# Ten of eighteen gather matrices made on ScalarE as reciprocal roots, and a first hop that adds both halves of a value while it scatters

## The chip, the cores and the metric

The kernel runs on one core of one Trainium2 chip. It is one launch on one core with these engines: TensorE (PE in the profile; PEld are its weight loads), VectorE (DVE), ScalarE (ACT), GpSimd (POOL) and SyncE (SP), which here mostly issues transfers. Each engine works through its own instructions in the order in which the program lists them. The metric is the time of the launch in device microseconds, as the median of several runs.

## The reference

The input is a graph with 10,000 nodes, 160,000 edges and 128 features per node, and seven propagations ("hops") followed by a small transformer block over the eight resulting tokens of each node:

```python
h = x
toks = [x]
for _ in range(7):
    msg = h[src] * deg_inv_sqrt[src, None] * deg_inv_sqrt[dst, None]
    h = _segment_sum(msg, dst, N)
    toks.append(h)
tok = jnp.stack(toks, axis=1)                      # (N, 8, D)
t = _layernorm(tok, axis=-1)
q, key, v = (jnp.einsum('nkd,de->nke', t, w) for w in (wq, wk, wv))
attn = _softmax(jnp.einsum('nkd,nld->nkl', q, key) * scale, axis=-1)
o = tok + jnp.einsum('nkd,de->nke', jnp.einsum('nkl,nld->nkd', attn, v), wo)
r = _layernorm(o, axis=-1)
alpha = _softmax(jnp.einsum('nkd,d->nk', r, w_r), axis=-1)
return jnp.einsum('nk,nkd->nd', alpha, o)
```

## The kernel before

**Representation.** The nodes form 79 blocks of 128. A hop is done by matrix products with zero-one matrices: for a block of destinations, TensorE first gathers the source rows of its edges and then scatters them, that is, adds them up by destination. The table of a hop (`tab`) holds each value as two f16 halves side by side, a leading part in columns 0 to 127 and the remainder in columns 128 to 255, so that a row has 256 columns. The edges of a block are sorted into cells of 32 places by the block of their source. Blocks 0 to 71 of the sources have a cell of their own each, four cells to a matrix, so there are `NG` = 18 gather matrices of 4 x 32 columns. One more scatter matrix (`NI` = 1) and an overflow matrix (`Sov`) take rows that are fetched from DRAM by index (`fetch`, lines 519 to 528).

**Stages.** (1) The first bucket pass (`pass_a`) counts and sorts the edges by destination block. (2) The second bucket pass takes the destination blocks in quads: `place` (lines 409 to 495) ranks the edges of four blocks into cells and writes their rows to DRAM (`srow`), and `matrices` (lines 497 to 516) makes the gather and scatter matrices of each block, stores them (`GSd`) for the later hops, and keeps them for the first hop, which runs in the same stage one quad later. (3) Hops two to seven read the stored matrices. (4) The attention follows.

**`matrices`.** For each block, SyncE reads the block's row of 2304 places to all 128 partitions (`rb`, one buffer, line 504). VectorE compares it with the partition number plus one (`pid1`), which gives the 18 gather matrices in one instruction of 2304 columns (line 511), and makes the 19 scatter matrices in another of 2432 columns (line 514). Then SyncE stores both (line 516). The transfer of the next row is issued after line 511.

**`block`.** A step gathers one or two matrices (line 580: four products of 32 columns of weights each, into a PSUM tile `p` of 128 x 512; there are three such tiles in the first hop), copies `p` to an f16 tile `e` on ScalarE (line 585) or VectorE (line 587, as a multiplication by a tile of ones), and two steps later scatters (line 556) with the scatter matrix as weights and `e` as the moving operand, into the accumulator `acc`. Nearly all copies of the first hop are ScalarE's; in later hops five of nine are. In the first hop `e` has a 257th column of ones, which counts the edges of each destination. When all 18 are added, the fetched rows follow (lines 542 to 569), VectorE adds the two halves of `acc` into `s` (line 571), and `fin` takes `s`. In the first hop `fin` is `fin1` (line 648): VectorE copies the count (line 649), ScalarE scales `s` for the next table (line 652) and for the token (line 623, into `r`, one buffer).

**Order.** The stage is written as three generators that are advanced in turn, 16 rounds to a quad (line 684 on): in each round a step of `place` of the next quad (in two rounds of three), a step of `matrices` (in one of four) and a step of the first hop of the quad before. The instructions get this order as their priority; a planner then fixes the order on each engine from its own estimates of times, moving forward what it takes to be ready. Transfers on SyncE's queue stand in order with their waits: the next row (line 504), the matrices (line 516), the token rows (line 627), the new table's rows (line 161).

Of the kernel before, what the change touches and what calls it, by code (L numbers as in the profile page):

```python
# [7 lines left out]
F32 = mybir.dt.float32  # L8
# [4 lines left out]
AF = mybir.ActivationFunctionType  # L13
ALU = mybir.AluOpType
# [5 lines left out]
NT = 79  # L20
NG = 18
NI = 1
CELL = 334
NK = 79
NR = 10240
# [14 lines left out]
class Hops:  # L40
    def __init__(self, ctx, dp, missing, tab, tc, x, src, dst, dis):
# [34 lines left out]
        self.one = cp.tile([128, 1], F32, name="one")  # L76
        V.memset(self.one, 1.0)
# [318 lines left out]
    def pb_open(self, c):  # L396
        tc, V = self.tc, self.nc.vector
        self.bwp = c.enter_context(tc.tile_pool(name="bw", bufs=2))
        self.bw1 = c.enter_context(tc.tile_pool(name="bw1", bufs=1))
        self.pU = c.enter_context(tc.tile_pool(name="pU", bufs=1, space=PSUM))  # L400
        self.psm = c.enter_context(tc.tile_pool(name="psm", bufs=1, space=PSUM))

        cp = self.bp
        es = cp.tile([NS, 4, NJ], I32, name="es")
        self.nc.gpsimd.iota(es, pattern=[[1, 4], [4, NJ]], base=0, channel_multiplier=-1)
        self.esel = cp.tile([NS, 4, NJ], F16, name="esel")
        V.tensor_scalar(self.esel, es, 0.0, None, op0=ALU.is_equal)

    def place(self, ts, got):

# [85 lines left out]

    def matrices(self, ts, dsl, W):

        nc, V = self.nc, self.nc.vector

        def row(t):
            rb = self.bw1.tile([128, 4 * NG * CAP], F16, name="rb")
            r1 = self.srow[t:t + 1, :]
            nc.sync.dma_start(rb, bass.AP(tensor=r1.tensor, offset=r1.offset, ap=[[0, 128], [1, 4 * NG * CAP]]))
            return rb

        rb = row(ts[0])
        yield
        for g, t in enumerate(ts):
            w = self.gsp.tile([128, (NJ + NG) * 128], F8, name="w")  # L510
            V.tensor_scalar(w[:, NJ * 128:], rb, self.pid1, None, op0=ALU.is_equal, saturate=False)  # L511
            if t != ts[-1]:
                rb = row(t + 1)
            V.tensor_tensor(w[:, :NJ * 128].rearrange("p (j d) -> p j d", d=128), dsl[:, g, :, None].to_broadcast([128, NJ, 128]),  # L514
                            self.iof1[:, None, :].to_broadcast([128, NJ, 128]), op=ALU.is_equal, saturate=False)
            nc.sync.dma_start(self.GSd[t], w)
            W.append(w)
            yield
# [11 lines left out]
    def block(self, t, w, tab, og, pend, lag, runs, first, evac, fin, lead=False, late=False, mid=None, ahead=None,  # L530
              after=None):

        nc, V, A, T, G = self.nc, self.nc.vector, self.nc.scalar, self.nc.tensor, self.nc.gpsimd
        m = 257 if first else 256
        acc = []


        def fetched(i, start=False, stop=False):  # L540
            W = w[:, (NG + i) * 128:(NG + i + 1) * 128] if i < NI else self.Sov[:, t, :]
            T.matmul(acc[0][:, :256], W, og[i], start=start, stop=stop)  # L542
            if first:
                T.matmul(acc[0][:, 256:257], W, self.ones16, start=False, stop=False)

        def begin():
            acc.append(self.pacc.tile([128, 512], F32, name="acc", tag="acc"))
            for i in range(NI if late else NI + 1):
                fetched(i, start=i == 0)

        def scat(e, jj):
            if not acc:
                acc.append(self.pacc.tile([128, 512], F32, name="acc", tag="acc"))
            for j in range(e.shape[1]):
                J = 2 * jj + j
                T.matmul(acc[0][:, :m], w[:, J * 128:(J + 1) * 128], e[:, j, :m], start=first and J == 0,  # L556
                         stop=J == NG - 1 and not (first or late))
                if first and J == 0 and not lead:
                    for i in range(NI):
                        fetched(i)  # L560

        def close():
            if first:
                if lead:
                    for i in range(NI):
                        fetched(i)
                T.matmul(acc[0][:, 256:257], self.Sov[:, t, :], self.ones16, start=False, stop=False)
            if first or late:
                T.matmul(acc[0][:, :256], self.Sov[:, t, :], og[NI], start=False, stop=True)  # L569
            s = self.fp.tile([128, 128], F32, name="s")  # L570
            V.tensor_reduce(s, acc[0][:, 0:256].rearrange("p (h d) -> p d h", h=2), axis=X, op=ALU.add)  # L571
            fin(t, s, acc[0])

        def gather(jj):
            n = min(2, NG - 2 * jj)
            p = self.pg.tile([128, 2, 2, 128], F32, name="p")
            for j in range(n):
                for q in range(4):
                    s = 4 * (2 * jj + j) + q
                    T.matmul(p[32 * q:32 * q + 32, j], w[:, NJ * 128 + s * CAP:NJ * 128 + (s + 1) * CAP], tab[:, s, :], start=True, stop=True)  # L580
            e = self.ebuf[self.eb_i % len(self.ebuf)]
            self.eb_i += 1
            pv = p[:, :n].rearrange("p j h d -> p j (h d)")
            if evac(jj):
                A.copy(e[:, :n, 0:256], pv)  # L585
            else:
                V.tensor_tensor(e[:, :n, 0:256], pv, self.one[:, :, None].to_broadcast([128, n, 256]), op=ALU.mult)  # L587
            pend.append(lambda: scat(e[:, :n], jj))

        jj = 0  # L590
        for i, n in enumerate(runs):
            for _ in range(n):
                gather(jj)
                if jj == 0 and not first and not mid:
                    ahead(self.ebuf[(self.eb_i - 1) % len(self.ebuf)][:, 0, 0:1])
                jj += 1
            if mid:
                mid(0)
            if not first:
                begin()  # L600
                if mid:
                    ahead()
            while len(pend) > lag:
                pend.pop(0)()
            if mid:
                mid(1)
            if after:
                after()
            if i == len(runs) - 1:
                pend.append(close)  # L610
            yield
# [17 lines left out]
    def run(self, ctx, att, nhop=K):  # L629
        tc, nc, V, A, T, G = self.tc, self.nc, self.nc.vector, self.nc.scalar, self.nc.tensor, self.nc.gpsimd  # L630
        with ExitStack() as c:
# [14 lines left out]


            def fin1(t, s, acc):
                V.tensor_copy(self.indeg[:, t:t + 1], acc[:, 256:257])  # L649
                if not done:  # L650
                    fin1.y = self.fp.tile([128, 2, 128], F32, name="y2")
                A.activation(fin1.y[:, len(done), :], s, AF.Copy, scale=self.dis2[:, t:t + 1])
# [25 lines left out]
            for q in range(nq + 1):  # L678
# [619 lines left out]
```

## Time and profile before

| | us |
|---|---|
| time, median of 3 runs (lowest, highest) | 3996.6 (3993.74, 4000.15) |
| the profiled execution, its own time | 3999.62 |
| its span, first to last instruction | 3997.8 |
| VectorE busy, second bucket pass, 600.30 to 1105.65 us | 492.02 of 505.35 |
| ScalarE busy, the same stretch | 316.19 |

In the rows of the profile an instruction is given by line, engine and operation, then output and input by the program's names with their shapes and types, then how often it occurs. "Mean ns" is the length of one, while busy time counts overlapping instructions once, so that a queue of instructions of one kind can stand closer than its mean. Idle time is the time of that engine just before the instruction, and the name behind the arrow is what ended it. The ends of matmuls are modelled, so a busy TensorE is not a TensorE at its peak.

### The profile page before, as it was taken

The page shows a single profiled execution, that of the slowest core. Times are in us where ns is not written, and L with a number is a line of the kernel's source. Part 1 is how long each engine was busy: PE and PEld are TensorE (multiplying, and loading weights), DVE is VectorE, ACT ScalarE, POOL GpSimd, SP SyncE. Part 2 cuts the span into 40 slices and gives each one's busy share as a digit, 9 for nine tenths or more (in the row PEclk, how much of TensorE's full clock was granted, in tenths as well). Part 3 has the DMA queues.
Part 4 walks back from the last instruction along what each step waited for, and adds up shares of the span by engine and source line. Part 5 has one row for each costly group of instructions (what it writes and reads, how often), then busy time and mean ns, then how long its engine had stood idle before and what let it go on. Part 6 is the DMA issues. An engine that isn't in the chain of part 4 may idle for free.

```text
span 3997.8 us, 165094 instructions
## 1 busy us (share of the span) xinstructions
PE 3745.5 (94%) x69690; PEld 3031.4 (76%) x69690; DVE 3322.9 (83%) x6961; ACT 2724.5 (68%) x6830; POOL 1766.6 (44%) x2342
## 2 busy tenths in 40 slices
PE   6886799999989999999999999999999999999997
PEld 4665566666658888888888788878878887788885
DVE  8998999999977777777777777777766666999998
ACT  6884456666666666666666666666665658888884
POOL 0000333333335665666666566656656662222222
PEclk8998899999999999999999999999999999999998
DMA  3100445454556666666666666666656552222220
GB/s 104 32 2 1 134 151 154 149 162 143 156 168 189 201 201 193 202 203 200 193 202 202 185 202 202 202 189 198 202 184 205 186 183 77 74 74 76 78 78 13
DMA packets 321189, 594.93 MB, mean 149 GB/s; under 512 B 56183, under 2 KB 214101, under 8 KB 315189
## 3 DMA queue, kind: packets, MB, share of 16 engines
q1 hardware_dynamic: 282485, 506.62, 40.0%
q0 software_dynamic: 35392, 72.55, 6.3%
q8 instruction: 546, 8.95, 0.9%
q10 hardware_dynamic: 2560, 5.12, 0.4%
q14 instruction: 206, 1.69, 0.1%
HBM read 455.43 MB, written 128.67 MB: 146 GB/s over the span
## 4 chain that ended last, share of the span: by engine, by line
PE 71%; DVE 19%; ACT 4%; issue 2%; DMA 2%; POOL 0%; another core or an unknown queue 0%; SPq 0%; DVEq 0%; ACTq 0%; POOLq 0%
PE p L580 26%; PE acc L556 24%; PE acc L542 4%; DVE w L514 3%; PE pv L972 3%; PE po L983 3%; PE pu L961 3%; DVE ux L219 2%; DVE o L212 2%; ACT rs L340 2%; PE tb L440 2%; PE pt L951 1%; DVE oh L206 1%; DVE R L212 1%; DVE w L511 1%
## 5 line engine op out<-in xcount | busy, mean ns | idle before, releaser
L585 ACT CAST eb<-p 128x512 f16<-128x512 f32 x3065 | 1623.7, 596 | 645.4 <-PE p L580 404.3
L587 DVE TENSOR_TENSOR eb<-p,one 128x512 f16<-128x512 f32 x1912 | 1230.6, 685 | 332.2 <-PE acc L556 195.9
L580 PE MATMUL p<-tab,w 128*32 128x256 f16 x39816 | 1288.7, 274 | 44.2 <-issue 21.4
L556 PE MATMUL acc<-eb,w 128*128 128x256 f16 (+1 forms) x9954 | 1246.9, 274 | 8.4 <-DVE indeg L649 3.1
L580 PEld LDWEIGHTS <-w 128*32 128x32 fp8e4 x39816 | 1002.3, 96 | 261.3 <-issue 225.8
L556 PEld LDWEIGHTS <-w 128*128 128x128 fp8e4 x9954 | 954.3, 98 | 170.3 <-issue 54.9
L526 POOL DMA_INDIRECT og<-tabh,oidx x553 | 613.3, 1109 | 767.7 <-DVE vi L478 389.6
L526 POOL DMA_INDIRECT og<-tabd,oidx x541 | 586.3, 1084 | 640.2 <-PE acc L556 294.3
L625 POOL TENSOR_SCALAR r<-s,ctok 128x128 f32<-128x128 f32 x474 | 294.3, 621 | 47.7 <-DVE s L571 30.3
L616 ACT ACTIVATE tab<-s,c 128x128 f16<-128x128 f32 x395 | 158.6, 402 | 209.7 <-DVE eb L587 185.6
L617 DVE SCALAR_TENSOR_TENSOR tab<-s,c,tab 128x128 f16<-128x128 f32 x395 | 138.9, 352 | 180.8 <-issue 168.0
L571 DVE TENSOR_REDUCE s<-acc 128x128 f32<-128x256 f32 x553 | 228.7, 414 | 24.0 <-PE acc L569 11.2
L997 ACT ACTIVATE junk<-tab 128x128 f32<-128x128 f32 x625 | 245.1, 394 | 0.0
L340 ACT ACTIVATE rs<-iof,rb 128x128 fp8e4<-128x128 f32 x784 | 231.8, 389 | 0.3
L514 DVE TENSOR_TENSOR w<-dsl,iof 128x2432 fp8e4<-128x2432 f16 x79 | 211.5, 2678 | 0.0
L983 PEld LDWEIGHTS po<-v,pT 128*128 128x128 f32 x1250 | 159.5, 194 | 42.1 <-issue 27.7
L525 POOL COPY og<-eb 128x1 f16<-128x1 f16 x452 | 83.9, 186 | 241.7 <-ACT eb L585 241.7
L1055 POOL TENSOR_TENSOR p<-e,in 128x512 f32<-128x512 f32 (+1 forms) x40 | 40.8, 1020 | 321.0 <-DVE e L1053 321.0
L972 PE MATMUL pv<-Wv,xT 128*128 128x131 f32 x1250 | 176.7, 285 | 1.3 <-ACT xT L952 0.6
L983 PE MATMUL po<-v,pT 128*128 128x128 f32 x1250 | 167.0, 277 | 5.5 <-DVE tab L989 4.1
L972 PEld LDWEIGHTS pv<-Wv,xT 128*128 128x128 f32 x1250 | 154.2, 192 | 17.9 <-issue 8.8
L542 PE MATMUL acc<-og,w 128*128 128x256 f16 x553 | 156.8, 284 | 0.0
(285 smaller groups left out, 4611.9 us busy)
## 6 DMA issues: line engine op xcount, KB each, us to landing
w<-gsd SPq DMA_DIRECT2D x474, 592.0 KB
gsd<-w SPq DMA_DIRECT2D x79, 592.0 KB
rb<-srow SPq DMA_DIRECT2D x79, 576.0 KB
tok<-r SPq DMA_DIRECT2D x546, 64.0 KB
tab<-tok SPq DMA_DIRECT2D x273, 128.0 KB
tabd<-tab SPq DMA_DIRECT2D x396, 64.0 KB
og<-tabh,oidx POOLq DMA_INDIRECT x553
og<-tabd,oidx POOLq DMA_INDIRECT x541
```

Of the source, the lines that this page charges most:

```text
L340: A.activation(ro[:, j - a, i, :], self.iof, AF.Abs_reciprocal_sqrt, scale=2.0 ** 21, bias=rb[:, j - VP, i:i + 1], saturate=False)
L514: V.tensor_tensor(w[:, :NJ * 128].rearrange("p (j d) -> p j d", d=128), dsl[:, g, :, None].to_broadcast([128, NJ, 128]), self.iof1[:, None ...
L526: self.nc.gpsimd.indirect_dma_start(out=o, out_offset=None, in_=src[0] if i == NI else src[1], in_offset=bass.IndirectOffsetOnAxis(ap=self ...
L542: T.matmul(acc[0][:, :256], W, og[i], start=start, stop=stop)
L556: T.matmul(acc[0][:, :m], w[:, J * 128:(J + 1) * 128], e[:, j, :m], start=first and J == 0, stop=J == NG - 1 and not (first or late))
L580: T.matmul(p[32 * q:32 * q + 32, j], w[:, NJ * 128 + s * CAP:NJ * 128 + (s + 1) * CAP], tab[:, s, :], start=True, stop=True)
L585: A.copy(e[:, :n, 0:256], pv)
L587: V.tensor_tensor(e[:, :n, 0:256], pv, self.one[:, :, None].to_broadcast([128, n, 256]), op=ALU.mult)
L625: self.nc.gpsimd.tensor_scalar(r, s, ct[:, t:t + 1], None, op0=ALU.mult)
L972: T.matmul(p[:, g - a, :], S[i]["xT"][:, g, :], Wv, start=True, stop=True)
L983: T.matmul(p[:, g - a, :], PT[i % 2][:, g, :], S[i]["v"][:, g, :128], start=True, stop=True)
L997: A.activation(j, S[i]["x"][:, g, :], AF.Square, bias=S[i]["x"][:, g, 0:1], scale=-1.0, accum_out=S[i]["sq"][:, g:g + 1])
```

## The change

A gather matrix entry becomes 1/4 instead of 1, and the copies that follow the gather multiply by 4. The first 10 of the 18 gather matrices (`NA` = 10, 1280 columns) are made on ScalarE in two pieces of 640 columns, as 1/sqrt(2^21 (row - p - 1) + 16): where the row's place equals the partition that is 1/sqrt(16) = 1/4, elsewhere it rounds to zero in the fp8 output. VectorE makes the other 1024 columns with a comparison and a multiplication by 0.25 in one instruction. `matrices` yields after each of the two pieces, so it has three steps per block instead of one, and is advanced in three rounds of four. The next row's transfer is listed after both pieces.

The copies become an activation with the scale 4 on ScalarE and a multiplication by a tile of fours on VectorE, in all hops. In the first hop each scatter with 257 columns becomes two with the same weights, one with the remainder half and the ones (129 columns) and one with the leading half (128), both into the same 128 columns of `acc`; the fetched rows likewise. So `acc` holds the finished sum with the count in column 128, VectorE's addition of the halves is left out in the first hop, and `fin1` reads `acc` itself.

```diff
@@ pb_open
+        self.off = cp.tile([128, 1], F32, name="off")
+        V.tensor_scalar(self.off, self.pid1, -2.0 ** 21, 16.0, op0=ALU.mult, op1=ALU.add)
@@ matrices
+        cut = NJ * 128 + 4 * NA * CAP
...
             w = self.gsp.tile([128, (NJ + NG) * 128], F8, name="w")
-            V.tensor_scalar(w[:, NJ * 128:], rb, self.pid1, None, op0=ALU.is_equal, saturate=False)
+            V.tensor_scalar(w[:, cut:], rb[:, 4 * NA * CAP:], self.pid1, 0.25, op0=ALU.is_equal, op1=ALU.mult, saturate=False)
+            for a in range(NJ * 128, cut, 640):
+                A.activation(w[:, a:a + 640], rb[:, a - NJ * 128:a - NJ * 128 + 640], AF.Abs_reciprocal_sqrt, scale=2.0 ** 21,
+                             bias=self.off, saturate=False)
+                yield
             if t != ts[-1]:
                 rb = row(t + 1)
@@ block
+        def both(W, rows, start, ones):
+
+            T.matmul(acc[0][:, :128 + ones], W, rows[:, 128:256 + ones], start=start, stop=False, skip_group_check=True)
+            T.matmul(acc[0][:, :128], W, rows[:, :128], start=False, stop=False, skip_group_check=True)
...
+            if first:
+                both(W, og[i], False, 0)
+                T.matmul(acc[0][:, 128:129], W, self.ones16, start=False, stop=stop, skip_group_check=True)
+                return
...
-                T.matmul(acc[0][:, :m], w[:, J * 128:(J + 1) * 128], e[:, j, :m], start=first and J == 0,
-                         stop=J == NG - 1 and not (first or late))
+                if first:
+                    both(w[:, J * 128:(J + 1) * 128], e[:, j], J == 0, 1)
+                else:
+                    T.matmul(acc[0][:, :256], w[:, J * 128:(J + 1) * 128], e[:, j, :256], start=False, stop=J == NG - 1 and not late)
...
-                T.matmul(acc[0][:, 256:257], self.Sov[:, t, :], self.ones16, start=False, stop=False)
-            if first or late:
+                fetched(NI, stop=True)
+                fin(t, acc[0][:, :128], acc[0])
+                return
+            if late:
...
-                A.copy(e[:, :n, 0:256], pv)
+                A.activation(e[:, :n, 0:256], pv, AF.Copy, scale=4.0)
             else:
-                V.tensor_tensor(e[:, :n, 0:256], pv, self.one[:, :, None].to_broadcast([128, n, 256]), op=ALU.mult)
+                V.tensor_tensor(e[:, :n, 0:256], pv, self.four[:, :, None].to_broadcast([128, n, 256]), op=ALU.mult)
@@ fin1
-                V.tensor_copy(self.indeg[:, t:t + 1], acc[:, 256:257])
+                V.tensor_copy(self.indeg[:, t:t + 1], acc[:, 128:129])
@@ run
-                    if i % 4 == 0:
+                    if i % 4 < 3:
                         next(mt, None)
```

More of the change, by code (lines that the diff above doesn't have):

```diff
@@ L22 @@
 NI = 1
+NA = 10
 CELL = 334
@@ L75, in __init__ @@
         V.memset(self.ones32, 1.0)
-        self.one = cp.tile([128, 1], F32, name="one")
-        V.memset(self.one, 1.0)
+        self.four = cp.tile([128, 1], F32, name="four")
+        V.memset(self.four, 4.0)
         self.ones16 = cp.tile([128, 1], F16, name="ones16")
@@ L497, in matrices @@
     def matrices(self, ts, dsl, W):
-        nc, V = self.nc, self.nc.vector
+        nc, V, A = self.nc, self.nc.vector, self.nc.scalar
+        cut = NJ * 128 + 4 * NA * CAP
         def row(t):
```

3 lines of the change are left out of this document (removed).

## The prediction

> **What bounds the kernel now.** I first cut the span into its stages with the view of busy time by stretch. Each row is a stretch in us and its length, then busy us (and instructions) of the matmul row of TensorE, its weight loads, VectorE, ScalarE, GpSimd, then granted clock, DMA share, GB/s.
>
> ```profile
> 0.00:400.00 400.00, 301.99 (x3385) 233.18 (x3385) 368.37 (x440) 289.36 (x948) 5.91 (x25) 0.89 0.12 35
> 437.57:600.30 162.73, 138.65 (x2360) 102.58 (x2359) 153.38 (x224) 86.28 (x193) 50.23 (x28) 0.92 0.45 142
> 600.30:1105.65 505.35, 462.20 (x8232) 340.39 (x8229) 492.02 (x716) 316.19 (x689) 184.55 (x105) 0.99 0.49 153
> 1105.65:1136.40 30.75, 27.99 (x532) 20.63 (x529) 29.75 (x49) 18.95 (x42) 11.92 (x8) 1.00 0.55 166
> 1136.40:1165.00 28.60, 24.46 (x420) 14.62 (x415) 23.85 (x31) 20.71 (x42) 12.12 (x8) 1.00 0.87 297
> 1200.00:3290.00 2090.00, 2065.99 (x42934) 1738.42 (x42929) 1573.73 (x3191) 1384.53 (x2728) 1288.38 (x1847) 0.99 0.63 197
> ```
>
> The first row lies in the first bucket pass, the last in hops two to seven, where TensorE is busy 98.8% of the time. The rows from 437.57 to 1136.40 us are the second bucket pass with the first hop, 18 quads of node blocks; the long one holds 13 whole quads: 52 blocks, 9.72 us each. VectorE is busy 9.46 us per block there (97%), ScalarE 6.08. The chain of work for that stretch names VectorE too.
>
> ```profile
> by line: DVE w L514 20.4%; DVE ux L219 8.2%; PE tb L440 8.1%; DVE R L212 8.0%; DVE w L511 6.7%; DVE ohp L206 6.1%; PE acc L556 5.7%; issue 4.8%; DVE rob L206 4.0%; PE ur L421 3.8%; PE p L580 3.5%; DVE oh L206 3.1%; ACT eb L585 2.2%; PE ur L
> ```
>
> So a microsecond of VectorE is nearly a microsecond of the stage, as long as nobody else is late. The groups of the same stretch (busy us, mean ns, idle before them and who ended it):
>
> ```profile
> L585 ACT CAST eb<-p 128x512 f16<-128x512 f32 x468 | 253.9, 590 | 86.8 <-PE p L580 78.7 <-PE acc L556 1.7 <-ACT eb L585 0.3
> L556 PE MATMUL acc<-eb,w 128*128 128x257 f16 x936 | 152.2, 277 | 3.8 <-ACT eb L585 1.3
> L514 DVE TENSOR_TENSOR w<-dsl,iof 128x2432 fp8e4<-128x2432 f16 x52 | 139.2, 2676 | 0.0
> L511 DVE TENSOR_SCALAR w<-rb,pid 128x2304 fp8e4<-128x2304 f16 x52 | 73.2, 1407 | 0.0
> L440 PE MATMUL tb<-R,oh 128*76 128x64 f16 x1300 | 56.4, 207 | 17.0 <-DVE R L212 17.0
> L219 DVE TENSOR_TENSOR ux<-oh,U 128x3800 f16<-128x3800 f16 x26 | 55.2, 2124 | 0.0
> L421 PE MATMUL ur<-oh,id 128*128 128x152 f16 x650 | 49.1, 229 | 0.0
> L206 DVE TENSOR_TENSOR rob<-rk,io 128x1600 f16<-128x1600 f16 x26 | 25.4, 978 | 0.0
> L571 DVE TENSOR_REDUCE s<-acc 128x128 f32<-128x256 f32 x52 | 21.2, 408 | 0.0
> L652 ACT ACTIVATE y<-s,dis 128x128 f32<-128x128 f32 x52 | 21.1, 405 | 54.7 <-DVE s L571 54.7
> ```
>
> **VectorE, per block.** In the timeline of one quad, what counts is start to start:
>
> ```profile
> 600.30 1.42 DVE L511 TENSOR_SCALAR w<-rb,pid 128x2304 fp8e4<-128x2304 f16 x1
> 609.16 1.41 DVE L511 TENSOR_SCALAR w<-rb,pid 128x2304 fp8e4<-128x2304 f16 x1
> 615.83 1.41 DVE L511 TENSOR_SCALAR w<-rb,pid 128x2304 fp8e4<-128x2304 f16 x1
> 617.16 0.41 DVE L571 TENSOR_REDUCE s<-acc 128x128 f32<-128x256 f32 x1
> 617.49 0.14 DVE L649 COPY indeg<-acc 128x1 f32<-128x1 f32 x1
> 623.25 1.41 DVE L511 TENSOR_SCALAR w<-rb,pid 128x2304 fp8e4<-128x2304 f16 x1
> ```
>
> The gather matrix (L511) occupies 1.33 us, the sum of halves (L571) 0.33. L206 and L219 rise by 0.52 ns per element (1600 to 3800: 978 to 2124), L514 by 1.04. L511 fits the faster slope: 1407 - 2304 x 0.52 = 209 ns fixed. Its remainder has 1024 columns: 209 + 532 = 741 ns, 0.66 start to start, so 0.67 is saved. It now has a second operation. Whether that costs anything is shown by two forms of the decode stage, L387 with two operations and L388 with one:
>
> ```profile
> L387 DVE TENSOR_SCALAR t<-t 128x2000 int32<-128x2000 int32 x1 | 1.2, 1196 | 0.0
> L388 DVE TENSOR_SCALAR t<-t 128x2000 int32<-128x2000 int32 x1 | 1.2, 1195 | 0.0
> ```
>
> It costs nothing there. If this one fell to L514's slope, it would be 209 + 1065 = 1274 ns and save 0.13; that end stays for the range. L571 goes wholly: 0.33. VectorE falls to 9.46 - 0.67 - 0.33 = 8.46 us per block.
>
> **ScalarE, per block.** It gains two pieces of 640 columns with a per-partition bias. Nearest forms, over the whole run:
>
> ```profile
> L340 ACT ACTIVATE rs<-iof,rb 128x128 fp8e4<-128x128 f32 x784 | 231.8, 389 | 0.3
> L157 ACT ACTIVATE tab<-y,q 128x256 f16<-128x256 f32 x39 | 19.5, 500 | 0.0
> L157 ACT ACTIVATE tab<-tab,q 128x2560 f16<-128x2560 f32 x3 | 7.1, 2412 | 0.0
> L429 ACT CAST U<-ur 128x152 f16<-128x152 f32 x40 | 11.5, 287 | 8.3 <-PE ur L427 8.3
> L317 ACT ACTIVATE U<-U 128x158 f16<-128x158 f32 x25 | 7.0, 286 | 9.0 <-PE U L309 5.4 <-issue 3.6
> 108.68 9.46 ACT L340 ACTIVATE rs<-iof,rb 128x128 fp8e4<-128x128 f32 x32
> ```
>
> L340 is the same function with the same kind of bias and the same output type. L157 rises by 0.83 ns per column, so 640 columns take 500 + 384 x 0.83 = 819 ns. The last row (timeline) shows 32 of L340 in 9.46 us, 0.29 apart, 0.10 under their mean: two pieces occupy 2 x 0.72 = 1.44 us. The function was used in the first pass, so I cost no table load. The copies become activations with a constant scale: L317 against L429 shows the two forms level from PSUM, so zero (ends: -0.03 and +0.05 each, nine per block here, five in later hops). L652 and L623 read PSUM instead of SBUF: zero, with 0.1 us either way. ScalarE rises to 7.5 us, and it loses its wait for L571: 54.7 us above, 1.05 per block, in which the copies behind it stood too. It still fits in what VectorE needs, and that is the cover; without it each piece would hold copies, and gathers behind three PSUM tiles, by up to 0.72 us.
>
> **TensorE, per block.** Twenty products (18 scatters, fetched rows, overflow) become two passes of half the columns, each with its own weight load.
>
> ```profile
> 768.00 1.05 PE L556 MATMUL acc<-eb,w 128*128 128x257 f16 x8
> 769.81 1.81 PE L421 MATMUL ur<-oh,id 128*128 128x152 f16 x25
> 784.16 2.02 PE L440 MATMUL tb<-R,oh 128*76 128x64 f16 x50 [0.43 <-DVE R L212]
> ```
>
> Less the last one's length, passes lie (1.05 - 0.28)/7 = 110 ns apart at 257 columns, (1.81 - 0.23)/24 = 66 at 152, (2.02 - 0.21)/49 = 37 at 64. At 128 a pass lies between 37 and 66; on the line between the two, 58. Two cost 116 against 110: 20 x 6 = 0.12 us per block; the top end, 132 against 110, gives 0.44. TensorE's need: a block of a later hop is 92 matmuls, so 42934/92 = 467 blocks in 2090 us, 4.48 us; the bucket pass adds 12.5 x 66 + 25 x 37 ns, eight passes of 250 columns at about the 110 of 257, and small ones, 2.9 us together. With the split that is 7.5, hidden under VectorE. Successive products into the same columns are nothing new: L440 does 25 of them.
>
> The Trainium skill, "TensorE: Matmul & The Clock Gate", section "Back-to-back issue gap", says that a stream of weight load and matmul pairs sustains about 81 ns per matmul at 128 columns. The rows speak against it: L421 moves 152 columns, with a load each, at 66. By that page the split would cost 20 x (162 - 110) = 1.04 us instead of 0.12.
>
> **The moved wait.** The row buffer `rb` exists once. SyncE's transfer of the next row (L504) waited for L511; now it also waits for ScalarE's second piece, in program order a step later. Behind it in SyncE's queue stand the matrix store, token rows and table rows; ScalarE's `r` (one buffer) would wait for a token store held up there. After the last placement VectorE meets rows in flight:
>
> ```profile
> 1143.90 0.67 SPq L504 DMA_DIRECT2D rb<-srow  x1
> 1149.30 1.42 DVE L511 TENSOR_SCALAR w<-rb,pid 128x2304 fp8e4<-128x2304 f16 x1 [1.96 <-DMA rb<-srow]
> 1150.75 0.32 SPq L504 DMA_DIRECT2D rb<-srow  x1
> 1155.98 1.42 DVE L511 TENSOR_SCALAR w<-rb,pid 128x2304 fp8e4<-128x2304 f16 x1 [1.58 <-DMA rb<-srow]
> ```
>
> From issue to reader it is 5.2 to 5.4 us; I take 5.3. Four rows per quad: today 4 x (5.3 + 1.33) = 26.5 of 38.9 us. With the pieces back to back behind one step's copies (a sixteenth of a quad has 2.25 copies, about 1.4 us with what else ScalarE does) and 0.3 for SyncE: 4 x (5.3 + 0.3 + 1.4 + 1.44) = 33.8 us. Still inside.
>
> **The sum.** VectorE at 8.46 us sets the pace. Today it idles 0.26 per block; with ScalarE at 7.5 and TensorE at 7.5 beside it I take 0.45: 8.91 per block, 0.81 less. Between 437.6 and 1136.4 us the stage does 18 quads, 71 blocks: -57.5. Before them four matrices are built without a hop, 0.67 off each: -2.7. In the stretch from 1136.40 to 1165.00 (four matrices without placement) rows are the bound and are given back about 0.6 later, three times: +2. Later hops, first pass and attention: zero; in the hops ScalarE has a third of its time free (1384.53 of 2090). Sum: -58. The profiled execution took 3999.6 us around its span of 3997.8, so 3941; it lies 3.0 above the median of the runs, so against that 3939. I say 3940. Its own range: at today's idle the gain is 1.0 x 71 (3925), with no idle at all 1.26 x 71 = 89 (3907); with L511 at the slow slope 0.46 x 71 = 33 (3964).
>
> **The rivals.**
> - Slower: the row loop becomes the bound. If the second piece keeps its place a whole step (38.9/16 = 2.4 us) behind the first, a quad needs 4 x (5.3 + 0.3 + 1.4 + 2.4 + 0.72) = 40.5 us against 38.9: +1.6 x 18 quads = +29, 4026. It decides from 4.4 us between landing and release (38.9/4 - 5.3). ScalarE would stand at the row with the copies queued behind it. For: L511 was one instruction, this is two with a hop step between. Against: the planner moves ready work forward, since L511 stands at 8.9, 6.7 and 7.4 us spacing in a quad instead of 9.7. Chance 0.17.
> - The same loop partly in the way: the second piece half a step behind, rows released 3.7 us after landing, 37.2 us per quad: 1.7 x 18 = 30 off, 3967, and up to 3996 as the delay nears 4.4. Against it the same. Chance 0.12.
> - The multiply drops L511 to the slow slope: 3964. Against: L387. Chance 0.05.
> - Half passes cost three quarters of whole ones, 82 ns of 110: 20 x 54 ns = 1.1 us, TensorE at 8.5, level with VectorE. Two in-order engines that wait for each other would then need about 9.2: 0.5 x 71 = 36 off, 3961. No row speaks for it; against it L421. Chance 0.04. The Trainium skill's sentence on pairs of 128 columns, above, would speak for it.
>
> **How the numbers follow.** The forecast has 0.62; 0.62 + 0.17 + 0.12 + 0.05 + 0.04 = 1. About 0.2% (8 us) is what a measurement of this kernel can tell from no change. Slower is the first rival, 0.17; within 0.2% a third of the second, 0.04; the rest is faster, 0.79. The range runs from 3912, close to the no-idle end, to 3990, which takes in most of the second rival and leaves the first out.
>
> **What would show it.** In the changed profile L511's successor at 128x1024 takes about 0.74 us and the new activations about 0.82; L571 is gone from the first hop only, with ScalarE's wait for it; VectorE is busy 8.5 us per block at 94 to 97%; a block takes 8.9; the copies stay at 590 and hops two to seven at their length. I am wrong if ScalarE or VectorE waits for `rb` in most quads, if quads take 38 us or more, if the new scatters show more than 70 ns per pass, or if the copies grow and the later hops lengthen.

## The result, and the profile after

The changed kernel takes 3977.88 us (3968.98 to 3980.77, 5 runs) against 3996.6 before: ratio 0.995, 95% interval 0.9935 to 0.9965. It is faster, by 19 us, where the prediction said 57. The time lies in the range and on the side that was forecast; the size was a third of the forecast.

Both profiled executions are cut at the same marks: the store of the second quad's rows (`srow`), the last such store (18 quads and 71 blocks later), and the end of hop 1. The busy time by stretch, first of the kernel before, then of the changed one (columns as in the prediction; the last row of each is the stretch behind the last store):

```profile
436.74:1135.22 698.48, 628.47 (x11106) 463.56 (x11106) 674.65 (x986) 420.90 (x924) 245.75 (x138) 0.97 0.49 151
1135.22:1184.16 48.94, 42.91 (x734) 26.05 (x733) 37.17 (x60) 33.87 (x72) 15.89 (x12) 1.00 0.60 200
```

```profile
432.19:1107.82 675.63, 623.91 (x12383) 487.85 (x12380) 616.85 (x914) 506.50 (x1056) 236.58 (x137) 0.97 0.48 156
1107.82:1164.48 56.66, 49.84 (x1044) 35.35 (x1043) 32.32 (x53) 44.76 (x91) 20.13 (x14) 1.00 0.52 176
```

| stretch | before, us | after, us | difference | forecast |
|---|---|---|---|---|
| up to the second quad's store | 436.74 | 432.19 | -4.5 | -2.7 |
| 18 quads | 698.48 | 675.63 | -22.9 | -57.5 |
| last store to the end of hop 1 | 48.94 | 56.66 | +7.7 | +2 |
| the rest (hops two to seven, attention) | 2813.6 | 2811.6 | -2.0 | 0 |

Nearly all of the miss lies in the 18 quads (34.6 us), most of the rest in the last stretch (5.7). Per block (a 71st of the stretch) VectorE's busy time fell from 9.50 to 8.69 us, 0.81 of the 1.0 that was forecast; its idle time rose from 0.34 to 0.83 us, where 0.45 was forecast. VectorE is busy 91% of the stretch instead of 97%. In the last stretch, which is longer, more is left to do: its matmuls rose from 734 to 1044, and the split adds only some 180 of them (groups L548 and L549, x162 each, where one scatter stood, and 18 for the fetched rows).

The single durations came out as forecast. The groups of the changed kernel in the 18 quads:

```profile
L522 DVE TENSOR_TENSOR w<-dsl,iof 128x2432 fp8e4<-128x2432 f16 x71 | 190.4, 2682 | 0.0
L517 ACT ACTIVATE w<-rb,off 128x640 fp8e4<-128x640 f16 x142 | 114.4, 832 | 43.6 <-DMA rb<-srow 43.3 <-PE acc L549 0.2
L207 DVE TENSOR_TENSOR oh<-kB,io 128x3800 f16<-128x3800 f16 x35 | 74.7, 2134 | 27.3 <-PE tb L443 27.3
L515 DVE TENSOR_SCALAR w<-rb,pid 128x1024 fp8e4<-128x1024 f16 x71 | 53.5, 753 | 6.8 <-DMA rb<-srow 6.7
L670 ACT ACTIVATE y<-acc,dis 128x128 f32<-128x128 f32 x70 | 26.2, 374 | 8.3 <-DVE indeg L667 7.3 <-issue 0.5
```

L515, the comparison with its second operation, takes 753 ns (741 forecast), L517, a ScalarE piece, 832 ns (819 forecast). What is new is on the right: ScalarE stands 43.3 us for the row, and VectorE 27.3 us before the placement's one-hot `oh`. VectorE's waits in the 18 quads (total us, times, longest), before and after:

```profile
DVE oidx L459 <- ACT dsl L458: 13.3, 16, 1.3
DVE tab L158 <- ACT tab L157: 3.1, 4, 0.8
DVE oh L206 <- PE tb L440: 2.6, 1, 2.6
```

```profile
DVE oh L207 <- PE tb L443: 27.3, 22, 2.3
DVE ux L220 <- ACT U L432: 9.2, 7, 2.2
DVE w L515 <- DMA rb<-srow: 6.7, 10, 1.9
DVE rk L228 <- PE ur L225: 3.8, 4, 1.8
```

`oh` has two buffers, and TensorE's count `tb` (L443) is the last reader of one. Before, VectorE stood there once; now it does so 22 times.

The passes of a split scatter on TensorE, ten in a row in the timeline (the first and the last shown):

```profile
705.45 0.23 PE L548 MATMUL acc<-eb,w 128*128 128x129 f16 x1
...
705.97 0.22 PE L549 MATMUL acc<-og,Sov 128*128 128x128 f16 x1
```

Nine gaps in 0.52 us are 58 ns each, the forecast's number. The Trainium skill, "TensorE: Matmul & The Clock Gate", section "Back-to-back issue gap", has about 81 ns for a pair of weight load and matmul at 128 columns; the trace does not agree. The copies of hops two to seven (window from 1200 to 3290 us, before, then after) are nearly level, 597 and 602 ns:

```profile
L585 ACT CAST eb<-p 128x512 f16<-128x512 f32 x2333 | 1228.2, 597 | 494.9 <-PE p L580 276.6 <-PE acc L556 195.4 <-remote 8.4
```

```profile
L603 ACT ACTIVATE eb<-p 128x512 f16<-128x512 f32 x2338 | 1241.1, 602 | 492.6 <-PE p L598 264.6 <-PE acc L573 197.9 <-remote 20.8
```

So the question was where about 35 us of VectorE's freed time went: its idle time in the quads rose from 23.8 to 58.8 us, and the wait for `tb` is 24.7 of these 35.

### The profile page after: what moved, and what is told of

It reads as the page before. It is cut to its first block, busy times and chain, and to the rows that moved or that the text cites. A ratio compares the mean times of both kernels' runs of the same rounds, so it can differ in the third digit from the quotient of the medians.

```text
span 3976.1 us, 168366 instructions
## 1 busy us (share of the span) xinstructions
PE 3742.6 (94%) x71270; PEld 3061.4 (77%) x71270; DVE 3254.0 (82%) x6883; ACT 2835.3 (71%) x6988; POOL 1761.4 (44%) x2342
## 4 chain that ended last, share of the span: by engine, by line
PE 70%; DVE 18%; DMA 5%; ACT 4%; issue 2%; another core or an unknown queue 0%; SPq 0%; DVEq 0%; ACTq 0%; POOL 0%; POOLq 0%
PE p L598 27%; PE acc L573 23%; PE acc L558 4%; DMA rb<-srow 3%; DVE o L213 2%; PE pv L990 2%; PE po L1001 2%; DVE oh L207 2%; PE pu L979 2%; DVE ux L220 2%; DVE w L522 2%; PE tb L443 1%; PE acc L548 1%; DVE st L1096 1%; PE pt L969 1%
## 5 line engine op out<-in xcount | busy, mean ns | idle before, releaser
L603 ACT ACTIVATE eb<-p 128x512 f16<-128x512 f32 x3065 | 1637.2, 602 | 573.9 <-PE p L598 326.4
L605 DVE TENSOR_TENSOR eb<-p,four 128x512 f16<-128x512 f32 x1912 | 1231.6, 686 | 343.4 <-PE acc L573 200.9
L573 PE MATMUL acc<-eb,w 128*128 128x256 f16 x8532 | 1013.1, 273 | 0.0
L573 PEld LDWEIGHTS <-w 128*128 128x128 fp8e4 x8532 | 836.5, 98 | 98.8
L534 POOL DMA_INDIRECT og<-tabh,oidx x553 | 627.0, 1134 | 642.0 <-DVE vi L481 388.8
L534 POOL DMA_INDIRECT og<-tabd,oidx x541 | 566.5, 1047 | 750.6 <-PE acc L573 290.5
L548 PE MATMUL acc<-eb,w 128*128 128x129 f16 x1422 | 218.0, 224 | 8.6 <-ACT eb L603 8.1
L549 PE MATMUL acc<-eb,w 128*128 128x128 f16 x1422 | 214.3, 222 | 0.2 <-issue 0.2
L589 DVE TENSOR_REDUCE s<-acc 128x128 f32<-128x256 f32 x474 | 196.9, 415 | 20.3 <-PE acc L587 10.3
L548 PEld LDWEIGHTS <-w 128*128 128x128 fp8e4 x1501 | 140.2, 99 | 69.0 <-issue 66.4
```

What stands on the lines that cost most here:

```text
L534: self.nc.gpsimd.indirect_dma_start(out=o, out_offset=None, in_=src[0] if i == NI else src[1], in_offset=bass.IndirectOffsetOnAxis(ap=self ...
L548: T.matmul(acc[0][:, :128 + ones], W, rows[:, 128:256 + ones], start=start, stop=False, skip_group_check=True)
L573: T.matmul(acc[0][:, :256], w[:, J * 128:(J + 1) * 128], e[:, j, :256], start=False, stop=J == NG - 1 and not late)
L603: A.activation(e[:, :n, 0:256], pv, AF.Copy, scale=4.0)
L605: V.tensor_tensor(e[:, :n, 0:256], pv, self.four[:, :, None].to_broadcast([128, n, 256]), op=ALU.mult)
```

## The experiments

The runs fall into four groups, each on a chip of its own with the kernel before beside it. Ratios hold within a group; the kernel before took 3995.12 us in group 1, 3940.37 in group 2, 3940.17 in group 3 and 3996.63 in group 4. "First chip" in the expectations is that of group 1, "second chip" that of group 3. The last two columns are of one profiled execution each, which lies up to 9.9 us from the median of its run (two_rows_old 9.9 and no_addition 7.0 above, matrices_split 6.8 below). The same changed kernel took 675.63 us for the 18 quads in the first profile and 671.63 in changed_third.

| group | run | median us | ratio to before (95%) | 18 quads, us | VectorE busy in them |
|---|---|---|---|---|---|
| 1 | two_rows | 3972.58 | 0.9941 (0.9928, 0.9955) | 667.21 | 620.08 |
| 1 | two_rows_old | 3996.67 | 1.0005 (0.9996, 1.0014) | 702.54 | 675.09 |
| 1 | halves_only | 3999.59 | 1.001 (1.0001, 1.0019) | 701.61 | 659.00 |
| 1 | matrices_only | 3967.79 | 0.9937 (0.9923, 0.9951) | 662.50 | 631.03 |
| 2 | split_only | 3944.12 | 1.001 (1.0002, 1.0019) | 679.79 | 673.79 |
| 2 | no_addition | 3933.16 | 0.9978 (0.9968, 0.9989) | 675.50 | 654.86 |
| 2 | matrices_15 | 3965.22 | 1.0062 (1.0049, 1.0075) | 694.80 | 620.04 |
| 2 | matrices_two_rows | 3921.49 | 0.9955 (0.9942, 0.9967) | 658.75 | 634.68 |
| 3 | changed_again | 3937.53 | 0.9995 (0.9986, 1.0004) | 665.77 | 615.44 |
| 3 | matrices_again | 3919.42 | 0.995 (0.9936, 0.9963) | 653.54 | 631.76 |
| 3 | matrices_split | 3936.84 | 0.9993 (0.9984, 1.0002) | 662.49 | 634.58 |
| 3 | matrices_no_addition | 3930.76 | 0.9976 (0.9967, 0.9985) | 661.83 | 613.74 |
| 4 | changed_third | 3977.79 | 0.9951 (0.9937, 0.9965) | 671.63 | 616.27 |
| 4 | changed_three_onehots | 3968.71 | 0.9926 (0.9913, 0.994) | 666.59 | 614.53 |
| 4 | matrices_three_onehots | 3980.62 | 0.9958 (0.9944, 0.9972) | 674.15 | 631.43 |
| 4 | changed_with_dead_sum | 3984.44 | 0.997 (0.996, 0.9979) | 673.25 | 635.88 |

**Is it the row?** The first suspect was the prediction's own rival: ScalarE stands at the one row buffer with the copies behind it. A second buffer takes that wait away, in the changed kernel and, as a control, in the kernel before:

```diff
-            rb = self.bw1.tile([128, 4 * NG * CAP], F16, name="rb")
+            if t % 2 or 56 <= t < 4 * NG:
+                rb = self.bw1.tile([128, 4 * NG * CAP], F16, name="rb")
+            else:
+                rb = self.tab[1][:, 60:69, :].rearrange("p t w -> p (t w)")
```

> The changed kernel with a second row buffer: rows of even blocks, except blocks 56 to 71, are read into a part of the next table that is not yet written. Theory A (ScalarE stands at the row: 27.6 us in 12 quads of the changed profile, with the placement's copies queued behind it): that wait nearly goes, a quad falls from 38.05 to about 36, and the time to 3935 to 3955. Theory B (VectorE's gaps are the latency of the placement's own chain, from its sorted rows through TensorE's counts back to the next one-hot, which the removed work used to cover): the row wait goes as well, but the time stays within 10 us of the changed kernel's 3978.

> The kernel before with the same second row buffer, as control. Both theories: VectorE was full there (97%) and met a row in flight for hardly any time, so it stays within 8 us of 3997. If it fell by more than that, the row was in the way before the change as well.

The control does nothing (1.0005). The changed kernel comes to 3972.58 us, 22.5 under before instead of 19: far from theory A's 3935 to 3955, and within theory B's 10 us. (The changed kernel itself was not run on this chip, and the intervals of the two ratios overlap.) ScalarE's waits in the 18 quads, of the changed kernel and of two_rows:

```profile
ACT w L517 <- DMA rb<-srow: 43.3, 37, 2.7
ACT eb L603 <- PE p L598: 40.6, 75, 2.6
ACT tbs L444 <- PE tb L443: 32.0, 27, 2.7
ACT H L425 <- PE ur L424: 22.3, 17, 1.9
```

```profile
ACT tbs L444 <- PE tb L443: 43.5, 33, 2.2
ACT H L425 <- PE ur L424: 34.4, 28, 1.8
ACT eb L606 <- PE p L601: 33.4, 66, 2.8
ACT w L520 <- DMA tab<-srow: 17.1, 13, 2.7
...
ACT w L520 <- DMA rb<-srow: 5.2, 7, 1.6
```

The wait for the row fell from 43.3 to 22.3 us, and the waits for TensorE's results in the placement (L444, L425) rose from 54.3 to 77.9. So the row takes a small part at most; its wait moves elsewhere.

**Which half of the change loses it?** The two parts were run apart: the sums of halves in TensorE alone (`block` and the count's column as changed, matrices and copies as before), and the gather matrices alone (matrices and copies as changed; one scatter of 257 columns and the addition as before).

> Only the first hop's half: both halves added into 128 columns, no addition of halves on VectorE; gather matrices all on VectorE, copies as before. VectorE loses 0.33 us per block, ScalarE its wait for that addition. By VectorE's need alone: 71 x 0.33 = 23 us off, 3973. Theory A: all of the 23, since no engine but VectorE reads the row. Theory B: less than half of it, 3985 to 3993.

> Only the gather matrices on ScalarE, with the copies times 4; the first hop's accumulator of 257 columns and VectorE's addition of the halves as before. VectorE loses 0.67 us per block, by its need alone 71 x 0.67 = 47 us off, 3949. Theory A: the row wait of about 2.3 us a quad, 18 quads, takes 41 of it, 3985 to 3995. Theory B: VectorE keeps more work to cover the chain than in the changed kernel, so more than half of the 47 comes, 3960 to 3972.

The matrices alone give 27 us, as theory B had it and more than the whole change (group 3, below, has both on one chip). The halves alone cost 4 us, where both theories had a gain. The 18 quads of matrices_only, and of halves_only:

```profile
432.51:1095.01 662.50, 620.68 (x11062) 446.12 (x11061) 631.03 (x985) 516.27 (x1058) 245.92 (x138) 0.98 0.49 159
```

```profile
435.12:1136.73 701.61, 641.58 (x12463) 506.92 (x12465) 659.00 (x921) 411.84 (x924) 269.12 (x138) 0.96 0.48 151
```

With the matrices alone VectorE's busy time falls by 0.61 us a block (0.67 forecast) and its idle time rises only from 0.34 to 0.44: 36 us less in the quads, where 0.67 a block is 47. That half of the forecast nearly holds there. Behind the last store, though, the stretch to the end of hop 1 is 58.6 us instead of 48.9, and the run as a whole gains 27. In halves_only VectorE has 15.65 us less to do in the quads and the quads are 3.1 us longer.

Then the halves were cut into their own two parts on the kernel before: two passes into separate columns, for all scatters but a block's first, with the addition kept (split_only), and one scatter of 257 columns with the addition left out (no_addition). Beside them, the matrices with 15 of 18 on ScalarE, advanced in every round, and the matrices with the second row buffer.

```diff
@@ split_only, scatters (fetched rows likewise)
-                T.matmul(acc[0][:, :m], w[:, J * 128:(J + 1) * 128], e[:, j, :m], start=first and J == 0,
-                         stop=J == NG - 1 and not (first or late))
+                    T.matmul(acc[0][:, 128:257], w[:, J * 128:(J + 1) * 128], e[:, j, 128:257], start=False, stop=False)
+                    T.matmul(acc[0][:, :128], w[:, J * 128:(J + 1) * 128], e[:, j, :128], start=False, stop=False)
@@ no_addition
+            if first:
+                fin(t, acc[0][:, 0:128], acc[0])
+                return
@@ matrices_15
-NA = 10
+NA = 15
-                    if i % 4 < 3:
+                    if True:
```

> The kernel before, with every scatter of the first hop but the first of a block, and its fetched rows, cut into two passes of half the columns; the halves stay in columns of their own and VectorE adds them as before. Theory C (the doubled passes cost the time, on TensorE or through the order that the planner makes of them): 10 to 25 us slower than before, 4005 to 4020. Theory D (the passes are free, since two lie 111 ns apart in the changed profile where one took 110; what is lost is VectorE's freed time, which waits eat): within 6 us of 3995.

> The kernel before without VectorE's addition of the halves in the first hop, scatters of 257 columns as before. It leaves out the remainder half: the first hop's result is its leading half alone, read by ScalarE from the accumulator. Theory C: VectorE's 0.33 us per block come back in full, 71 x 0.33 = 23 us off, 3972. Theory D: as in the run with the halves alone, within 8 us of 3995.

> Only the matrices on ScalarE, 15 of 18 in three pieces (four steps per block, one in each round), the addition of halves kept. VectorE was busy 97.6% with 10 of 18, so if its need still rules, its 640 columns (0.33 us per block) give 23 us more: 3945. If ScalarE's queue now rules (0.72 us per block more on 81% busy), nothing more comes or some is given back: 3965 to 3985.

> Only the matrices on ScalarE, 10 of 18, with the second row buffer. If ScalarE's stand at the row (22 us in 500 us there) reaches VectorE, 8 to 15 us come off 3968; if VectorE's need rules, as its 97.6% says, it stays within 6 us of 3968.

On the kernel before, where VectorE is full, the two passes cost 4 us and the missing addition gives 7, a third of the 23 us of work that goes: both within theory D. The second row buffer adds nothing to the matrices (0.9955, against 0.995 without it in group 3). With 15 matrices on ScalarE the kernel is 25 us slower than before, where even the worse of the two forecasts had a gain of 10. Its 18 quads, and VectorE's largest wait there:

```profile
435.06:1129.86 694.80, 628.82 (x11001) 445.15 (x11001) 620.04 (x983) 554.52 (x1125) 203.62 (x137) 0.96 0.48 152
```

```profile
DVE w L515 <- DMA rb<-srow: 35.4, 31, 2.6
```

VectorE has 15 us less to do than in matrices_two_rows of the same group and idles 74.8 us instead of 24.1. ScalarE is busy 80% there, no more than that, and rows now hold VectorE for 35.4 us: the mechanism of the prediction's slower rival, one step further along the same change. That is read from the waits; a second row buffer was not tried with 15.

**On top of the matrices.** Group 3 put each part of the halves on the matrices, with the changed kernel and the matrices beside them.

> The changed kernel once more, so that the four corners (addition kept or left out, scatter in one pass or two, with ten matrices on ScalarE in each) stand on one chip. 15 to 25 us below the kernel before, as before.

> The matrices alone once more: 18 to 30 us below the kernel before, and 4 to 12 us below the changed kernel.

> Ten matrices on ScalarE, scatters cut into two passes into columns of their own, VectorE's addition kept. Theory E (the two passes are what gives time back once VectorE is no longer full): 8 to 15 us slower than the matrices alone. Theory F (the missing addition gives it back: ScalarE reads the accumulator itself and its fixed order changes): within 4 us of the matrices alone.

> Ten matrices on ScalarE, scatters of 257 columns, no addition: the remainder half is left out of the first hop's result. Theory E: 5 to 20 us faster than the matrices alone, since VectorE is 97% busy there. Theory F: no faster than the matrices alone, up to 12 us slower.

Here the matrices give 21 us, and each part of the halves takes some of it back: the two passes 17.4 us, the missing addition 11.3, both together 18.1, which leaves the changed kernel level with the one before (15 to 25 us below it was expected). The passes cost more than theory E's 15, and the missing addition costs time, as theory F had it and against theory E. The missing addition is the telling one: it adds no work and takes some from VectorE (ScalarE then reads the accumulator itself, so the waits between the engines change with it). The 18 quads and VectorE's largest waits, of matrices_again and then of matrices_no_addition:

```profile
432.57:1086.11 653.54, 612.41 (x11039) 442.88 (x11035) 631.76 (x985) 516.21 (x1058) 237.08 (x137) 0.99 0.49 161
```

```profile
DVE oidx L462 <- ACT dsl L461: 8.3, 10, 2.4
DVE w L515 <- DMA rb<-srow: 4.6, 5, 1.4
```

```profile
431.09:1092.92 661.83, 616.04 (x11017) 443.40 (x11013) 613.74 (x916) 504.24 (x1056) 237.90 (x136) 0.98 0.49 159
```

```profile
DVE oh L207 <- PE tb L443: 15.0, 14, 1.4
DVE w L515 <- DMA rb<-srow: 11.3, 15, 1.6
```

VectorE has 18.0 us less to do and the quads take 8.3 us more: its idle time rises from 21.8 to 48.1 us. The largest of the new waits is the one for `tb`, which matrices_again does not have in its list at all. The timeline shows why it can be absent. For each pair of blocks VectorE makes the one-hot `oh`, then `ux`, then the ranks `rob`, from which TensorE gets its counts `tb`. In the changed kernel (VectorE):

```profile
831.19 2.14 DVE L220 TENSOR_TENSOR ux<-oh,U 128x3800 f16<-128x3800 f16 x1 [1.61 <-ACT U L432]
833.73 2.14 DVE L207 TENSOR_TENSOR oh<-kB,io 128x3800 f16<-128x3800 f16 x1 [0.40 <-PE tb L443]
...
841.14 0.98 DVE L207 TENSOR_TENSOR rob<-rk,io 128x1600 f16<-128x1600 f16 x1
...
846.14 2.14 DVE L207 TENSOR_TENSOR oh<-kB,io 128x3800 f16<-128x3800 f16 x1 [0.89 <-PE tb L443]
```

In matrices_again:

```profile
817.30 2.12 DVE L220 TENSOR_TENSOR ux<-oh,U 128x3800 f16<-128x3800 f16 x1
...
823.66 0.98 DVE L207 TENSOR_TENSOR rob<-rk,io 128x1600 f16<-128x1600 f16 x1
...
830.49 2.13 DVE L207 TENSOR_TENSOR oh<-kB,io 128x3800 f16<-128x3800 f16 x1
```

In matrices_again the one-hot behind a pair's ranks (830.49) is the next pair's. In the changed kernel the next pair's stands ahead of those ranks already (833.73), and the one behind them (846.14) is for the pair after next, ahead even of the next pair's `ux` (858.72). Its buffer is the one that TensorE's counts for the present pair still have to read, and all of VectorE's later work stands behind it.

In the 18 quads the changed kernel lists 24 of its 35 one-hots so early, ahead of the `ux` of the pair before, and 21 of them wait for `tb`. In matrices_again it is one, without a wait; in the kernel before two, one of them with a wait; in matrices_no_addition 18, 14 of them with a wait. The early place alone does not make the wait: in no_addition, on the kernel before, 18 stand as early and none waits. Taken by six quads each, the changed kernel falls short of the forecast gain (a third of 57.5, or 19.2 us) by 6.2, 19.1 and 9.4 us, with 0.9, 15.7 and 10.6 us of waits for `tb`.

**Is it that buffer, and does VectorE's time count at all?** Theory G held that the two one-hot buffers eat the gain, theory H that waits would only move. Group 4 gave a third buffer to every third pair of the first 12 of the 18 quads, in the changed kernel and in the matrices alone, and put a useless addition back into the changed kernel:

```diff
@@ changed_three_onehots, matrices_three_onehots
+            if (ts[0] // 2 + p0 // 2) % 3 == 2 and ts[0] < 48:
+                oh = self.tab[1][:, 55:70, :].rearrange("p t w -> p (t w)")[:, :NCH * NS * 2].rearrange("p (c k i) -> p c k i", k=NS, i=2)
+                V.tensor_tensor(oh, cols(self.kB)[:, :, None, :].to_broadcast([128, NCH, NS, 2]),
+                                self.io2[:, None, :NS, :].to_broadcast([128, NCH, NS, 2]), op=ALU.is_equal)
+            else:
+                oh = self.onehot(wp, "oh", cols(self.kB), NS)
@@ changed_with_dead_sum
+                d = self.fp.tile([128, 128], F32, name="dead")
+                V.tensor_reduce(d, acc[0][:, None, 0:128].to_broadcast([128, 2, 128]).rearrange("p h d -> p d h"), axis=X, op=ALU.add)
```

> The changed kernel as it stands, for comparison on the same chip: 17 to 19 us under the kernel before on the first chip, 3 us on the second.

> The changed kernel with a third buffer for the one-hot (oh) of the placement, laid into a part of tab[1] that hop 1 has not reached, for every third pair of blocks up to block 47 (12 of the 18 quads). In the last run of the changed kernel VectorE's next one-hot stood 24.3 us for TensorE's counts tb in the window 600 to 1080 us, since both buffers were still in use. Theory G (these two buffers are what eats the time that VectorE gains): the time falls by 12 to 20 us against the changed kernel. Theory H (the wait only moves on to the next link between TensorE, ScalarE and VectorE, because the fixed order on the engines leaves each of them late in turn): within 5 us of the changed kernel, and the waits for tb turn up at the next reader.

> The gather matrices alone (10 on ScalarE, addition kept, 257 columns) with the same third one-hot buffer. There VectorE did not stand for tb at all. G and H: within 5 us of the gather matrices alone, some 21 us under the kernel before on the second chip and 27 us on the first. Well below that would say that a second buffer is short there as well.

> The changed kernel with one VectorE addition a block put back whose sum nobody reads (the first half of the accumulator added to itself, 0.41 us busy, 0.33 us on the engine). If VectorE's time bounded the changed kernel it costs 71 x 0.33 = 23 us. If the time that the halves free on VectorE is spent in waits (G and H): 0 to 6 us.

For the quads the dead sum is the clearest answer. The 18 quads of changed_third, then of changed_with_dead_sum with its added line:

```profile
433.78:1105.41 671.63, 619.68 (x12381) 485.57 (x12378) 616.27 (x914) 506.00 (x1056) 238.88 (x136) 0.98 0.49 157
```

```profile
434.74:1107.99 673.25, 619.45 (x12392) 487.93 (x12388) 635.88 (x984) 507.83 (x1057) 219.27 (x136) 0.98 0.48 157
```

```profile
L585 DVE TENSOR_REDUCE dead<-acc 128x128 f32<-128x256 f32 x70 | 29.0, 414 | 0.7 <-PE acc L556 0.7
```

VectorE is busy 19.6 us longer and the quads take 1.6 us more; its idle time falls from 55.4 to 37.4. So in the changed kernel VectorE's time no longer sets the pace of the quads: the added work took up time that had been waiting. Its order differs too: 18 of the 35 one-hots stand early instead of 24, and the wait for `tb` is 6.3 us, where changed_third has 26.4.

The run as a whole is 6.7 us slower than changed_third (the intervals just overlap), a little over the 0 to 6 of G and H and far under 23. In the two profiled executions most of the difference lies behind the last store, 64.1 us against 56.2, with no more matmuls there (1034 against 1050); why is open. The same addition, left out of the kernel before, gave 7 us, so by whole runs its price is not shown to have changed.

With the third one-hot buffer the changed kernel gains 9 us (the intervals just overlap), between what G (12 to 20) and H (within 5) expected. But VectorE's wait for `tb` did not go. Its largest waits there (L422 is the one-hot in the third buffer):

```profile
DVE oh L207 <- PE tb L448: 20.9, 16, 2.1
...
DVE tab L422 <- PE tb L448: 4.4, 4, 1.3
```

That is 25.3 us against 26.4 in changed_third: with the third buffer 13 of the 35 one-hots are listed yet one pair earlier, and 11 of these wait. Nor does the gain lie where the waits were. Against changed_third the first six quads are 6.7 us shorter, with 0.9 us of waits for `tb` in changed_third and 1.0 here; the next six 0.9 us shorter, with 14.8 and 12.4; the last six, which have no third buffer, 2.5 us longer. So G's cause does not hold, and where the 9 us come from is not shown.

In the matrices alone, which had next to no such wait, the run with the same buffer was slower, where within 5 us was expected: 0.9958 where the matrices gave 0.9937 in group 1, on a chip on which the kernel before takes the same. The 18 quads are 674.15 us against 662.50, and all of that lies in the last six, which have no third buffer (238.90 against 226.68). An edit that adds no work and takes away no wait of note went with a difference of some 8 us by the ratios (the intervals overlap a little, and the chips differ); that the planner's other order does it is argued, not shown. Differences under some 10 us between two edits here are therefore not put down to one mechanism.

What stays open is whether the loss on top of the matrices is the planner's order or the length of the chain between the engines (ranks on VectorE, counts on TensorE, copies on ScalarE). The old order with the new instructions was not tried.

## Why the prediction was right or wrong

- **VectorE bounds the stage now: right for the kernel before, and the error was to keep it as the bound to the end.** The matrices, the larger part, gave 36 of the 47 us in the quads that a full VectorE promises, and 27 in the run (21 on another chip). After that VectorE's time was no longer the pace of the quads (dead sum: 19.6 us more work, 1.6 us more time), and the prediction's sum went on charging it.
- **L511 to 0.66 us, second operation free: right.** 753 ns; busy time per block fell 0.61 in matrices_only, 0.67 forecast.
- **"L571 goes wholly: 0.33" as a gain of 0.33 per block: this step failed.** It was counted at 23 us. On a full VectorE it gave 7 (no_addition), and with the split a loss of 4 (halves_only); on top of the matrices it cost 11.
- **"I take 0.45" of idle time per block: the mis-sized term.** It measured 0.83. With the busy time (8.69 instead of 8.46) it makes up the 35 us: 71 x (0.38 + 0.23) = 43, less 71 x 0.12 = 8 for the starting point, which over the 18 quads was 9.84 us a block, not the 9.72 of the thirteen. The higher busy time fits the waits: an instruction that starts after one counts its whole length, where in a queue it overlaps its neighbour (L511: 1.41 long, 1.33 start to start).
- **ScalarE's pieces at 0.72 occupied, 7.5 us in all: right in price.** 832 ns each; busy 7.13 us a block. Its wait for L571 (54.7 us in the thirteen quads) went as said, but waits for the row and for TensorE took its place.
- **TensorE's split at 58 ns per pass: right, and the rival of 82 ns is out.** Yet the two passes cost 4 us alone and 17 on the matrices, where 0.12 us a block would be 8.5: TensorE's own time was counted, the later start of what stands behind it in order was not. That this is what costs is argued, not shown.
- **Copies and later hops at zero: right**, 597 and 602 ns, the rest 2 us shorter.
- **The row loop (the slower rival and the one partly in the way): there, but small.** ScalarE waits 43.3 us for `rb`; with half of that freed the kernel took 5 us less (two_rows, on another chip, the intervals overlapping). It decides only with 15 matrices on ScalarE. The prediction's sign of error, "if ScalarE or VectorE waits for `rb` in most quads", came true (37 waits of ScalarE, some in each of the 18 quads) without being the main cause.
- **The last rows, +2: mis-sized**, +7.7. Part of it is hop work that the quads pushed behind the last store, so quads and tail together gained 15 us.
- **The range held the time; the likeliest case (3907 to 3964) did not.** Its upper part was there for a row loop partly in the way, which is not what took the time: that the range held is luck.

## What to carry to other kernels

A busy engine is a bound only until the change has made room on it: cost each part of a change on the kernel as the parts before it leave it, not each on the old one. With engines that meet in a fixed order, the first 0.6 us a block taken from a VectorE at 97% shortened the quads by 0.5 us a block here, and the next 0.2 came back as waits. Where a planner makes the order, run the parts apart before adding them: the gather matrices alone took 3919.42 us where the changed kernel took 3937.53 (group 3), and came to 0.9937 in group 1, with half of the change left away.

## What was not expected of the hardware

- The same program differs by 1.4% from chip to chip: the kernel before took 3995.12 and 3996.63 us in groups 1 and 4, 3940.37 and 3940.17 in groups 2 and 3. The changed kernel's stretch behind hop 1 was 2811.6 us on one chip and 2777.1 on another. The gain differs as well: 0.995 and 0.9951 on the first kind, 0.9995 on the other. The kernel before was not profiled on the faster chips, so where that comes from is open.
- Two ScalarE pieces follow each other at less than their length, as the prediction took from L340. In the timeline of the changed kernel two stand as 1.55 us, which is 0.72 apart:

```profile
1113.42 1.55 ACT L517 ACTIVATE w<-rb,off 128x640 fp8e4<-128x640 f16 x2
```

The Trainium skill, "ScalarE: Activation LUTs", section "What ACT_TABLE_LOAD costs", gives 280 ns plus 0.833 ns per column for an activation with a bias per partition, an estimate of 813 ns for 640 columns, and an overlap of about 93 ns; the trace agrees (832 ns, 0.11 overlapped).
